# Gated attention and a low-rank mixer on one core: loads moved behind a transposition, first score pairs in two PSUM tiles, small steps in one burst

## The chip, the core and the metric

The kernel runs on one core of a Trainium2 chip. The metric is the device time of one execution in microseconds (us). The engines are called TensorE (PE in the profile, with PEld for its weight loads), VectorE (DVE), ScalarE (ACT), GpSimd (POOL) and SyncE (SP), whose queue issues nearly all DMAs.

## The reference

Batch 8, sequence S = 3136, width D = 256, key width 64, low rank 32, hidden width 1024.

```python
scores = (1.0 / S) * np.matmul(z, z.transpose(0, 2, 1))
attn = np.maximum(scores, 0.0) ** 2
x = u * np.matmul(attn, v)
h = x.transpose(0, 2, 1) @ U @ V
y = x + h.transpose(0, 2, 1)
out = y + np.maximum(y @ w_ch1, 0.0) @ w_ch2
```

The attention has no softmax: a score is scaled, rectified and squared. The low-rank part mixes over the whole sequence of a batch, so x + h of a batch can start only when all x of that batch are there. Inputs and output are fp32; the kernel's matmuls take bf16.

## The kernel before, in words

**Tiles and slots.** A batch has six groups of 512 rows (g = 0 to 5) and a small one of 64 rows (g = 6). A group is four tiles of 128 rows. The 56 pairs (batch, group) are worked one after the other, and the text calls each a slot: slot t = 7b + g. So slots 7, 14, 21, ... are the first of a batch and slots 6, 13, 20, ... the last. In slot t PE does the attention times v of its own group (`av_stream`, L644), the scores of later groups (`todo`), and, one batch behind, x + h of group t - 7 (`u2_unit`, L823) and both layers of group t - 8 (`ch1_part`, L922, and `ch2_stream`, L1010).

**Pairs over the row halves.** Nearly every matmul contracts over 64 rows, and two of them run side by side on the two halves of PE's rows, each into its own PSUM bank (`pair`, L179). A bank may pass from one half to the other only when the first has done with it; `post` (L170, the nop at L174) puts a nop on POOL that waits for that and tells PE. The loops thus run one "way" over a stretch, turn, and run the other way; score pairs are placed at the turn, where the nop is under way. A PSUM tile is two banks; there are four (`take_ps`, L148).

**Scores.** A block is 512 keys by 512 rows in bf16, made by two jobs (h = 0 and 1) of two tiles each. `score_burst` (L538) does the matmuls, `rectify` (L366) chooses who scales and rectifies (ACT by an activation, or DVE), and a square on DVE follows (`square`, L362, the instruction at L364). In slot 0 the first jobs take their way from the list `ways` (L105): "half" lets ACT take one bank and DVE the other of the same PSUM tile, each rectifying and squaring its own. For batch 0 blocks are made for both sides of the diagonal at first; later a block above the diagonal is turned by a DMA transposition (`issue_turn`, L416).

**Small group.** `score_small` (L559) makes its scores, `av_small` (L703) its attention times v, with array tiles of 64 rows by 64 columns; `ch1_small` (L968) and `ch2_small` (L1090) are its two layers, the second with 64x64 tiles too. `four_sums` (L730) adds the four partial sums of these: a copy by ACT and two adds by DVE. `last_turn` (L551) turns the small group's attention for the other groups.

**Low-rank part.** `t1_all` (L792) sums U-transposed times x over the 25 tiles of a batch, with array tiles of 128 rows by 32 columns, then an ACT copy, a DVE add and a DVE copy. `u2_unit` multiplies by V, adds x on DVE, casts the sum to bf16 (for g = 0 on DVE, L886) and issues a DMA transposition of it, `x_turn` (L782, issue L785), into u2T. `ch1_part` reads u2T.

**Order.** The order is made by a planner that runs while the program is written. Its clock counts 256 columns of a pair as one unit (109 ns in the trace). `hold(due, f)` keeps a step until the clock has passed `due`; `run_held` (L124) runs what is ripe; `urgent` keeps block turns back from the time that a sum is cast until its turn is issued. Each engine works its queue in order, SP too. In a slot `emit` (L1110) walks the light units (96 pairs of attention times v, a unit each, then the second layer's) and puts other steps in by their place: an entry (place, need, turn, step) waits for `need` free PSUM tiles, up to 14 units or `hurry` more.

**Loads.** v and z of the next batch, u of the next group and, in the first slots, U, V, w_ch1 and w_ch2 (`first_loads`) come through staging tiles and are cast a slot later (`casts_next`, held again). In slots up to 7 the loads are held at 5, 27, 49, ... units after the slot's start and u at 60.

Of the kernel before, what the change touches and what calls it, by code (L numbers as in the profile page):

```python
# [18 lines left out]
def kernel(  # L19
# [82 lines left out]
    ready_turns = []  # L102
    urgent = []
    slot = [0]
    ways = ["half", "half", "both", "dve"]  # L105
    waiting = [0]

    def needed(e):
# [257 lines left out]
    def rectify(dst, src, b, part=1, whole=False):  # L366

        ready = clock[0] + 3
        dve, act = max(free_at["dve"], ready), max(free_at["act"], ready)
        if whole and slot[0] == 0:  # L370
            dve += 6.5 * waiting[0]
            ends = {"dve": dve + DVE, "act": act + 19, "both": max(act + 8.7, dve) + 7.5}
            given = bool(ways)
            way = ways.pop(0) if ways else min(ends, key=lambda w: ends[w])
            if way == "half":
                nc.scalar.activation(out=dst[:, 0], in_=src[:, 0], func=AF.Relu, scale=scale)
                nc.vector.tensor_scalar(  # L377
                    out=dst[:, 1], in0=src[:, 1], scalar1=scale, scalar2=0.0, op0=ALU.mult, op1=ALU.max
                )
                nc.scalar.activation(out=dst[:, 0], in_=dst[:, 0], func=AF.Square)  # L380
                nc.vector.tensor_tensor(out=dst[:, 1], in0=dst[:, 1], in1=dst[:, 1], op=ALU.mult)  # L381
                done = max(book("act", ready, 5.2), book("dve", ready, 6.2))
                return done, max(book("act", ready, 5.2), book("dve", ready, 3.5))
            if way == "dve":
                if not given:
                    run_held(ready + 9)
                return one_pass(dst, src, ready)
            if way == "act":
                nc.scalar.activation(out=dst, in_=src, func=AF.Relu, scale=scale)
                nc.scalar.activation(out=dst, in_=dst, func=AF.Square)  # L390
                done = book("act", ready, 8.7)
                book("act", ready, 8.7)
                return done, free_at["act"]
        elif dve + 8 * part < act:
            nc.vector.tensor_scalar(  # L395
                out=dst, in0=src, scalar1=scale, scalar2=0.0, op0=ALU.mult, op1=ALU.max
            )
            return book("dve", ready, 11.2 if part == 1 else 6.4), None
        nc.scalar.activation(out=dst, in_=src, func=AF.Relu, scale=scale)  # L399
        return book("act", ready, 8.7 if part == 1 else 5.3), None  # L400
# [36 lines left out]
    def score_pairs(jobs):  # L437
# [50 lines left out]
            )  # L488
        return made

    def score_finish(made):
        for dst, k, ps, turn, key in made:
            if key and split(*key):
                score_finish_split(dst, k, ps, turn, key)
                continue
            if turn:
                J, g, b = turn
                unturned[blocks[b, g, J][0]] = False
            done, whole = rectify(dst, ps, key[0] if key else 0, whole=True)
            ps_free[k] = done  # L500
            waiting[0] += whole is None

            def finish(dst=dst, turn=turn, key=key, whole=whole):
                if whole is None:
                    waiting[0] -= 1
                    square(dst)
                if key:
                    squared[key] = squared.get(key, 0) + 1
                if turn:
                    hold(clock[0] + (7 if whole is None else 1), lambda: ready_turns.append(turn))  # L510

            hold(whole or done, finish)

    def score_finish_split(flat, k, ps, h, key):
# [23 lines left out]
    def score_burst(jobs):  # L538
        score_finish(score_pairs(jobs))


    def place_of(jt):

# [662 lines left out]
    def load_V(i0):  # L1206
# [27 lines left out]
        3: lambda: load_V(0),  # L1234
        4: lambda: load_V(2),
        5: lambda: load_w(0),
        6: lambda: load_w(1),
    }


# [70 lines left out]
    clock[0] = 43  # L1311
    free_at.update(dve=46, act=47)
    jobs0 = jobs_of(0, 0)
    score_burst(jobs0[:1])
    score_burst(jobs0[1:2])
    score_burst(jobs0[2:3])
    clock[0] = 60

# [1 line left out]
    for b in range(B):  # L1320
        for g in range(NQ):
            t = b * NG + g - 1
            new = jobs_of(b, g)
            if g == 0 and b > 0:
                x, y = (5, 10) if b == 1 else (5, 11)
                todo[t - 2] += new[:x]
                todo[t - 1] += new[x:y]
                todo[t] += new[y:12] if b == 1 else new[y:]
                todo[t + 1] += new[12:] if b == 1 else []
            elif b == 0 and g == 0:  # L1330
                todo[0] += new[3:]
            elif b == 0 and g and g % 2 == 0:
                todo[t] += new[:-1]
                todo[t + 1] += new[-1:]
            else:
                todo[t] += new
# [5 lines left out]
    direct = (B - 1, 0)  # L1342

    def early(b, g):
        return b > 1 and g == NQ

    for t in range(n_items):
        slot[0] = t
# [8 lines left out]
        if t + 1 < n_items and t > NG and not early(*items[t + 1]):  # L1357
            load_u(*items[t + 1])
        if t > NG and g_now == NQ and b_next < B:
            hold(clock[0] + 60 + 70, lambda b=b_next: load_u(b, NQ))  # L1360
        if t == n_items - 3:
            xTs[direct] = take_block()[1][:, : GT // 2, :].rearrange("p a (q d c) -> p (a q) d c", d=ND, c=P)
            x_turn(*direct, xTs[direct])
        for i, f in enumerate(casts_next):
            hold(clock[0] + (90 if g_now == NQ and b_next > 1 else 60 if t == NG else 15 if t >= NQ else 45) + 12 * i, f)
        casts_next = []
        spare += spare_next
        spare_next.clear()
        steps = load_part(b_next, g_now) if b_next < B else []
        steps += first_loads[t]() if t in first_loads else []  # L1370

        def load(step):
            casts_next.extend(step())
# [1 line left out]
        for i, f in enumerate(steps):  # L1375
            if t > NG:
                load(f)
            else:
                hold(clock[0] + 5 + 22 * i, lambda f=f: load(f))
        if t <= NG:  # L1380
            hold(clock[0] + 60, lambda t=t: load_u(*items[t + 1]))
        if g_now == 0 and t:
            last_turn(att[0])
        if b_next < B and g_now == 2:
# [24 lines left out]
        if av and full:  # L1409

            last = nA - 9
            for h, x, y in zip(hs, (4, 22, 36, 62), (16, 32, 48, last)):
                qc.append((x, 1, False, one(h, 0)))
                qc.append((y, 0 if y == 32 else 1, y != 32, lambda h=h, y=y: (scores(y != 32), one(h, 1)())))
            n = len(mine) - 3
            qs += [(9 + 74 * i / n, 1, False, lambda: scores(1)) for i in range(n)]
        elif av:

            if mix:
                qc += [(x, 1 - way, False, lambda way=way: ch1_small(*mix, way, box1)) for way, x in ((0, 36), (1, 48))]  # L1420
            if fin:
                qc.append((72, 2, False, lambda: (ch2_small(*fin), av_small(att[0], NQ))))
            k = min(2, len(mine) // 3)
            n = len(mine) - 3 * k
            at = [1 + 80 * i / n for i in range(n)]
            if t == 0:
                at, k = [16, 30, 46, 50, 64, 68, 78, 84, 92], 0
                qs += [(4, 0, True, lambda: scores(1)), (12, 0, True, lambda: z_turn(0, 2 * GT, on_act))]
                qs += [(x, 0, True, lambda: scores(1)) for x in (24, 40, 56, 72, 88)]
                qm.append((20, 0, False, lambda: (cast_z(2, 0, on_dve), cast_z(2, 1, on_dve), book("dve", 0, 8))))  # L1430
                qm.append((34, 0, False, lambda: z_turn(0, 4 * GT, on_act)))
                qm.append((58, 0, False, cast_tail))
                qm.append((62, 0, False, lambda: z_turn(0, 6 * GT, on_act)))
            qs += [(x, 1, False, lambda: scores(1)) for x in at]
            qs += [(x, k, True, lambda: scores(k)) for x in (16, 48, nA - 2) if k]
        else:

            small = (lambda: None) if early(*att) else (lambda: av_small(*att))
            order = mine[:1] + [small] + mine[1:]
            if mix:  # L1440
                c0, c1, d0, d1, c2, c3, d2, d3 = parts(mix, box1)
                up = [lambda: u2_unit(*u2i)]
                if fin:
                    late = mine[-1:] if early(*att) else []
                    rest = mine[: len(mine) - len(late)]
                    order = [c0] + rest[:1] + [c1, d0, d1] + [c2] + rest[1:] + [c3, d2, d3] + up
                else:
                    order = up + [small, c0, c1, d0, d1, c2, c3, lambda: t1_all(att[0]), d2, d3]
            qc += [(0, 0, False, f) for f in order]


        if av and u2i:
            if u2i[1] == 0:
                qm.append((8, 1, False, lambda: t1_all(u2i[0])))
            qm.append((22 if u2i[1] == 0 else 40, 1, False, lambda: u2_unit(*u2i)))

        if not av:
            qm += [(nC // 2, -1, False, f) for f in late or [small]] if nC else []
# [72 lines left out]
```

## Time and profile before

| | |
|---|---|
| median of 3 runs | 982.09 us (981.95 to 982.22) |
| profiled execution, own time | 986.39 us |
| its span, first to last instruction | 984.6 us |
| mean granted TensorE clock | 0.998 |
| ACT `activation` of 128x1024 from PSUM (L399), each | 1.03 us |
| DVE square of 128x1024 (L364), each | 0.69 us |
| DVE add of `u2_unit` (L870), 128x1024, each | 1.22 us |
| landing of a turn of x + h (L785), least, median, most | 2.3, 3.6, 8.4 us |

In the timeline a row has its start, its duration, the engine, the line of the kernel, the operation, what is written and read, and in square brackets the engine's idle time before it with what ended it. Rows that follow one another with one meaning are merged (x4 is four instructions). "64*128 64x256" is a matmul on an array tile of 64 rows by 128 columns whose moving operand is 64x256. A row with SPq is the time that SP's queue took to issue a DMA, not its landing. Almost all matmuls come through the helper at L184.

### The profile page before, as it was taken

To read this page: it belongs to the slowest core of one execution; us is meant where nothing else is said; L and a number is where in the kernel's file an instruction comes from. 1 tells how busy PE (TensorE), PEld (TensorE's weight loads), DVE (VectorE), ACT (ScalarE), POOL (GpSimd) and SP (SyncE) were. 2 spreads that over 40 slices of the span, in tenths; PEclk is the share of its full clock that TensorE was granted. 3 is DMA by queue.
4 is the path that set the end of the run, shared out by engine and by line. 5 is a ranking of instruction groups with operands and counts; after the bars stand their busy time and mean duration, and the time that the engine had idled before them with its cause. 6 is when DMAs were issued, how large, how long until landed. Compare 5 with 4: busy or idle time off the path is not lost.

```text
span 984.6 us, 35373 instructions
## 1 busy us (share of the span) xinstructions
PE 973.7 (99%) x16163; PEld 773.4 (79%) x16163; DVE 628.2 (64%) x811; ACT 482.4 (49%) x565; POOL 15.2 (2%) x25
## 2 busy tenths in 40 slices
PE   8999899999999999999999999999999999999998
PEld 5788677877778778787777877788777887778766
DVE  6878755668556685566755667556775567653363
ACT  7877642456324473355633555334654346431353
POOL 4200000000000000000000000000000000000000
PEclk9999999999999999999999999999999999999999
DMA  8899999979997799987999879997799978965153
GB/s 269 193 225 192 228 196 188 223 153 197 195 204 167 160 192 192 205 170 170 185 208 207 154 178 179 223 189 153 173 207 206 194 144 163 186 135 95 55 114 99
DMA packets 372405, 176.37 MB, mean 179 GB/s; under 512 B 347296, under 2 KB 350624, under 8 KB 372256
## 3 DMA queue, kind: packets, MB, share of 16 engines
q1 hardware_dynamic: 372256, 174.12, 85.6%
q8 instruction: 126, 2.06, 0.9%
q14 instruction: 23, 0.19, 0.1%
HBM read 62.56 MB, written 25.69 MB: 90 GB/s over the span
## 4 chain that ended last, share of the span: by engine, by line
PE 96%; DVE 1%; ACT 1%; DMA 1%; issue 0%; DVEq 0%
PE ps L184 93%; PE ps L714 1%; DMA u2T<-x_bf 1%; PE ps L797 1%; ACT blk L399 0%; PE ps L1096 0%; DVE blk L364 0%; PE ps L1300 0%; PE ps L331 0%; DVE blk L377 0%; DVE blk L381 0%; DVE x_bf L749 0%; DVE blk L406 0%; DVE out_sb L870 0%; DVE blk L395 0%
## 5 line engine op out<-in xcount | busy, mean ns | idle before, releaser
L184 PEld LDWEIGHTS <-blk 64*128 64x128 bf16 x12288 | 609.7, 94 | 159.9 <-POOLq L174 9.6
L184 PE MATMUL ps<-v_bf,blk 64*128 64x256 bf16 x9216 | 613.0, 269 | 2.3 <-DVE blk L364 1.1
L399 ACT ACTIVATE blk<-ps 128x1024 bf16<-128x1024 f32 (+1 forms) x335 | 315.3, 970 | 346.6 <-PE ps L184 343.2
L364 DVE TENSOR_TENSOR blk<-blk 128x1024 bf16<-128x1024 bf16 x350 | 221.1, 656 | 49.1 <-ACT blk L399 48.4
L184 PE MATMUL ps<-u2T,w_bf 64*128 64x512 bf16 (+1 forms) x1792 | 227.9, 350 | 2.8 <-DMA u2T<-x_bf 2.8
L184 PE MATMUL ps<-w_bf,blk 64*128 64x256 bf16 x3072 | 192.0, 269 | 0.0
L959 DVE TENSOR_SCALAR blk<-ps 128x1024 bf16<-128x1024 f32 x105 | 128.5, 1224 | 97.6 <-PE ps L184 96.6
L962 ACT ACTIVATE blk<-ps 128x1024 bf16<-128x1024 f32 x87 | 88.3, 1022 | 119.0 <-PE ps L184 118.8
L184 PE MATMUL ps<-zzT 64*128 64x512 bf16 (+2 forms) x902 | 129.8, 327 | 0.6 <-ACT zzT L340 0.6
L184 PEld LDWEIGHTS <-w_bf 64*128 64x128 bf16 x1792 | 84.3, 94 | 30.2 <-POOLq L174 5.0
L749 DVE TENSOR_TENSOR x_bf<-ps,u_sb 128x1024 bf16<-128x1024 f32 x48 | 58.7, 1222 | 71.4 <-PE ps L184 71.4
L870 DVE TENSOR_TENSOR out_sb<-ps,x_bf 128x1024 f32<-128x1024 f32 x42 | 51.4, 1224 | 58.1 <-PE ps L184 58.1
L1082 DVE TENSOR_TENSOR out_sb<-ps,out_sb 128x1024 f32<-128x1024 f32 x42 | 51.4, 1224 | 18.6 <-PE ps L184 18.3
L184 PEld LDWEIGHTS <-zzT 64*128 64x128 bf16 x902 | 41.2, 94 | 6.9 <-ACT zzT L340 1.5
L184 PE MATMUL ps<-t_sb,V_bf 64*128 64x256 bf16 x200 | 20.6, 269 | 0.0
L395 DVE TENSOR_SCALAR blk<-ps 128x1024 bf16<-128x1024 f32 (+1 forms) x14 | 16.6, 1185 | 5.9 <-PE ps L184 5.1
L206 DVE CAST v_bf<-stage 128x1024 bf16<-128x1024 f32 (+1 forms) x30 | 18.5, 617 | 0.0
L184 PE MATMUL ps<-v_bf,last_sb 64*128 64x256 bf16 x192 | 18.5, 269 | 0.0
L204 ACT CAST v_bf<-stage 128x1024 bf16<-128x1024 f32 (+1 forms) x18 | 18.1, 1005 | 0.0
L206 DVE CAST x_bf<-out_sb 128x1024 bf16<-128x1024 f32 x22 | 15.2, 689 | 0.3
L1082 DVE TENSOR_TENSOR blk<-ps,blk 128x1024 f32<-128x1024 f32 x5 | 6.1, 1225 | 11.9 <-PE ps L184 11.8
L204 ACT CAST x_bf<-out_sb 128x1024 bf16<-128x1024 f32 x13 | 13.5, 1037 | 0.0
(83 smaller groups left out, 239.1 us busy)
## 6 DMA issues: line engine op xcount, KB each, us to landing
u_sb<-in_u_dram SPq DMA_DIRECT2D x48, 512.0 KB, 5.1
stage<-in_v_dram SPq DMA_DIRECT2D x42, 512.0 KB, 6.1
out_dram<-out_sb SPq DMA_DIRECT2D x42, 512.0 KB, 3.1
stage<-in_z_dram SPq DMA_DIRECT2D x7, 512.0 KB, 5.9
blk<-in_v_dram SPq DMA_DIRECT2D x5, 512.0 KB, 6.3
out_dram<-blk SPq DMA_DIRECT2D x5, 512.0 KB, 2.6
blk<-blk SPq DMA_TRANSPOSE x156, 5.1
blk<-in_moe_w_ch_dram SPq DMA_DIRECT2D x4, 512.0 KB, 4.9
```

The source lines that it names most:

```text
L184: ins = nc.tensor.matmul(**args)
L204: nc.scalar.copy(out=out, in_=in_)
L206: nc.vector.tensor_copy(out=out, in_=in_)
L364: nc.vector.tensor_tensor(out=a, in0=a, in1=a, op=ALU.mult)
L395: nc.vector.tensor_scalar(out=dst, in0=src, scalar1=scale, scalar2=0.0, op0=ALU.mult, op1=ALU.max)
L399: nc.scalar.activation(out=dst, in_=src, func=AF.Relu, scale=scale)
L714: nc.tensor.matmul(out=ps[c * hp : c * hp + rows, h, :D], lhsT=smalls[b][h * hp : (h + 1) * hp, place_of(jt), :], rhs=v_bfs[b][h * hp : (h ...
L749: nc.vector.tensor_tensor(out=xs[b, g][:rows, :n, :], in0=four(box["ps"])[:rows, :n, :], in1=u_sbs[b, g][:rows, :n, :], op=ALU.mult,)
L870: nc.vector.tensor_tensor(out=o[:rows, :n, :], in0=four(ps)[:rows, :n, :], in1=x, op=ALU.add)
L959: nc.vector.tensor_single_scalar(out=r, in_=ps[:, :, :gw], scalar=0.0, op=ALU.max)
L962: nc.scalar.activation(out=r, in_=ps[:, :, :gw], func=AF.Relu)
L1082: nc.vector.tensor_tensor(out=o, in0=acc, in1=o, op=ALU.add)
```

## The change

- `ways` loses its two "half" entries. The first two score jobs go through a new function, `shared_pairs`: it takes two PSUM tiles for both jobs, and in each job ACT reads a bank of the one and DVE a bank of the other.
- Blocks of batch 0 whose first job is made in slots 1 to 5 are squared as a whole, after their second job (`whole_block`).
- Loads: w_ch2 goes from slot 6 to slot 7; slot 7's loads are held at 78, 90, 102 and 114 units, w_ch2 first; u for slot 7 is loaded 5 units into slot 6, u for slot 8 at 88 units of slot 7; u of batch 1's small group comes 2 units into slot 7, that of later batches at 60 in place of 130 units. Casts of slot 8 are held at 45 units, those of slot 7 at 15.
- `av_small` of batch 1 moves from slot 13 to place 64 of slot 7.
- In slots 14, 21, ..., 49: `ch1_small` moves from places 36 and 48 to 3 and 10; `t1_all` from place 8, and `ch2_small` with `av_small` from place 72, to one step at place 22; `u2_unit` from place 22 to 36.
- In slots 13, 20, ..., 48: x + h of the small group comes first, then the eight first-layer parts without a score between them, then scores; two score jobs instead of one stand at the second layer's turn. From batch 2 on, two score jobs come from the slot before.

The diff, cut a little at its context:

```diff
-    ways = ["half", "half", "both", "dve"]
+    ways = ["both", "dve"]
...
-            if way == "half":
-                nc.scalar.activation(out=dst[:, 0], in_=src[:, 0], func=AF.Relu, scale=scale)
-                nc.vector.tensor_scalar(
-                    out=dst[:, 1], in0=src[:, 1], scalar1=scale, scalar2=0.0, op0=ALU.mult, op1=ALU.max
-                )
-                nc.scalar.activation(out=dst[:, 0], in_=dst[:, 0], func=AF.Square)
-                nc.vector.tensor_tensor(out=dst[:, 1], in0=dst[:, 1], in1=dst[:, 1], op=ALU.mult)
-                done = max(book("act", ready, 5.2), book("dve", ready, 6.2))
-                return done, max(book("act", ready, 5.2), book("dve", ready, 3.5))
...
+    halves, merged = {}, set()
+
+    def whole_block(n, key, turn):
+        waiting[0] -= 1
+        if n == 2:
+            square(blocks[key][1], 11.7)
+            squared[key] = 2
+        if turn:
+            hold(clock[0] + 7, lambda: ready_turns.append(turn))
...
+            if key and not key[0]:
+                n = halves[key] = halves.get(key, 0) + 1
+                if n == 1 and 0 < slot[0] < NQ:
+                    merged.add(key)
+                if key in merged:
+                    finish = lambda n=n, key=key, turn=turn: whole_block(n, key, turn)
             hold(whole or done, finish)
...
+    def shared_pairs(jobs):
+
+        (ka, a), (kb, d) = take_ps(), take_ps()
+        for i, (b, g, (J, h)) in enumerate(jobs):
+            zzT = zzTs[b]
+            if h == 0:
+                blocks[b, g, J] = take_block()
+            for jj in range(2):
+                key = J * GT + 2 * h + jj
+                nc.tensor.matmul(
+                    out=(a if jj == i else d)[:, jj, :],
+                    lhsT=half(zzT, jj, key * P, P),
+                    rhs=half(zzT, jj, groups[g][0], GW),
+                    start=True,
+                    stop=True,
+                )
+            pe(GW / 256)
+            dst = blocks[b, g, J][1][:, 2 * h : 2 * h + 2, :]
+            x, y = dst[:, i], dst[:, 1 - i]
+            nc.scalar.activation(out=x, in_=a[:, i], func=AF.Relu, scale=scale)
+            nc.vector.tensor_scalar(out=y, in0=d[:, 1 - i], scalar1=scale, scalar2=0.0, op0=ALU.mult, op1=ALU.max)
+            nc.scalar.activation(out=x, in_=x, func=AF.Square)
+            nc.vector.tensor_tensor(out=y, in0=y, in1=y, op=ALU.mult)
...
-        6: lambda: load_w(1),
+        NG: lambda: load_w(1),
...
-    score_burst(jobs0[:1])
-    score_burst(jobs0[1:2])
+    shared_pairs(jobs0[:2])
     score_burst(jobs0[2:3])
...
-                x, y = (5, 10) if b == 1 else (5, 11)
+                x, y = (5, 10) if b == 1 else (5, 9)
...
     def early(b, g):
-        return b > 1 and g == NQ
+        return b > 0 and g == NQ
...
         if t > NG and g_now == NQ and b_next < B:
-            hold(clock[0] + 60 + 70, lambda b=b_next: load_u(b, NQ))
+            hold(clock[0] + 60, lambda b=b_next: load_u(b, NQ))
+        if t == NG:
+            hold(clock[0] + 2, lambda: load_u(1, NQ))
...
-            hold(clock[0] + (90 if g_now == NQ and b_next > 1 else 60 if t == NG else 15 if t >= NQ else 45) + 12 * i, f)
+            hold(clock[0] + (90 if g_now == NQ and b_next > 1 else 45 if t == NG + 1 else 15 if t >= NQ else 45) + 12 * i, f)
...
-        steps += first_loads[t]() if t in first_loads else []
+        steps = (first_loads[t]() if t in first_loads else []) + steps
...
-                hold(clock[0] + 5 + 22 * i, lambda f=f: load(f))
+                hold(clock[0] + (78 + 12 * i if t == NG else 5 + 22 * i), lambda f=f: load(f))
         if t <= NG:
-            hold(clock[0] + 60, lambda t=t: load_u(*items[t + 1]))
+            hold(clock[0] + (5 if t == NQ else 88 if t == NG else 60), lambda t=t: load_u(*items[t + 1]))
...
-                qc += [(x, 1 - way, False, lambda way=way: ch1_small(*mix, way, box1)) for way, x in ((0, 36), (1, 48))]
+                qc += [(x, 1 - way, False, lambda way=way: ch1_small(*mix, way, box1)) for way, x in ((0, 3), (1, 10))]
+            if t == NG:
+                qc.append((64, 2, False, lambda: av_small(1, NQ)))
             if fin:
-                qc.append((72, 2, False, lambda: (ch2_small(*fin), av_small(att[0], NQ))))
+                qc.append((22, 2, False, lambda: (t1_all(u2i[0]), ch2_small(*fin), av_small(att[0], NQ))))
...
-                    late = mine[-1:] if early(*att) else []
+                    late = mine[-2:] if early(*att) else []
                     rest = mine[: len(mine) - len(late)]
-                    order = [c0] + rest[:1] + [c1, d0, d1] + [c2] + rest[1:] + [c3, d2, d3] + up
+                    order = up + [c0, c1, d0, d1, c2, c3, d2, d3] + rest
...
-            if u2i[1] == 0:
+            if t == NG:
                 qm.append((8, 1, False, lambda: t1_all(u2i[0])))
-            qm.append((22 if u2i[1] == 0 else 40, 1, False, lambda: u2_unit(*u2i)))
+            qm.append((40 if u2i[1] else 22 if t == NG else 36, 1, False, lambda: u2_unit(*u2i)))
```

## The prediction

> **What bounds the kernel.** I read the page's busy shares first, then PE's own waits, then the timeline around each of them.
>
> ```profile
> span 984.6 us, 35373 instructions
> ...
> PE 973.7 (99%) x16163; PEld 773.4 (79%) x16163; DVE 628.2 (64%) x811; ACT 482.4 (49%) x565; POOL 15.2 (2%) x25
> ```
>
> TensorE (PE) is the bound; no other engine comes near. The change adds and drops no matmul, so it can win only where PE stands still or is slow. A row's duration hides small pauses, since matmuls overlap; I therefore took the distance from each matmul's start to the next in the trace. Inside a stream, a pair over both row halves of 64x256 takes 109 ns and of 64x512 216 ns; whatever is above that is a pause. All pauses add up to 17.4 us: 6.2 in the first 20 us, 1.7 from 20 to 40, 4.4 from 100 to 120, and about 0.55 in each later batch. 17.4 us is thus the ceiling. PE's waits name the large ones:
>
> ```profile
> PE ps L184 <- DMA u2T<-x_bf: 2.8, 1, 2.8
> PE ps L184 <- DVE blk L364: 1.1, 2, 0.8
> ...
> PE ps L184 <- ACT blk L380: 0.8, 1, 0.8
> ...
> PE ps L184 <- DVE blk L381: 0.2, 1, 0.2
> ```
>
> (total us, times, longest.) The first is the wait of slot 8's first `ch1_part` for the turn of x + h. The timeline there:
>
> ```profile
> 100.39 0.50 SPq L226 DMA_DIRECT2D stage<-in_z_dram  x1
> 100.94 1.09 SPq L308 DMA_DIRECT2D u_sb<-in_u_dram  x2
> ...
> 102.25 0.69 DVE L886 CAST x_bf<-out_sb 128x1024 bf16<-128x1024 f32 x1
> ...
> 102.97 2.25 SPq L785 DMA_TRANSPOSE u2T<-x_bf  x1
> ...
> 111.45 1.04 PE L184 MATMUL ps<-u2T,w_bf 64*128 64x512 bf16 x4 [2.76 <-DMA u2T<-x_bf]
> ```
>
> The turn is issued at 102.97 and lands 8.44 us later; the other 54 turns of x + h land after 2.3 to 5.7 us. From 99.10 to 101.47 five loads of 512 KB each go out just before it (two of z, one of w, two of u), and the u loads land at 107.9 and 110.5: the turn stands behind them. The windows (last columns: granted clock, DMA share, GB/s) show the sequel:
>
> ```profile
> 102.00:109.00 7.00, 6.70 (x114) 5.35 (x108) 6.24 (x11) 5.06 (x6) 0.00 (x0) 1.00 1.25 315
> 109.00:116.00 7.00, 4.54 (x46) 2.85 (x48) 2.07 (x4) 1.79 (x3) 0.00 (x0) 0.76 0.91 202
> ```
>
> After the pause the clock is at half for 3.4 us; matmuls start 213 ns apart instead of 109, which costs 1.5 us more. The place costs 2.9 + 1.5 = **4.4 us**.
>
> **Part 1: loads behind the turn.** In slot 7 the loads of w_ch2, of z and of the next u are held to 78-114 units of 256 columns (about 8.5 to 12.4 us) after the slot's start; before, z went at 5 and 27, u at 60, and w_ch2 in slot 6. By the planner the turn is ripe near 70 units (`u2_unit` about 54, from 93.9 to 99.8 us; then its own 4, a delay of 3, 11.2 and 6.3 for DVE, less 6: 72), so SP gets it ahead of them. What is left before it in SP's queue is `last_turn`, the 64 KB of u for batch 1's small group, and a u load that now goes 50 units earlier. With the usual 3.2 to 5.7 us the turn lands at 106.2 to 108.7. PE wants it at 108.5, plus 1.5 us because `av_small` of batch 1 now runs in slot 7 (50 matmuls; 1.54 us in the chain, taken out of slot 13). Gain 4.4, unless SP or DVE is 1 us later than before. The later loads have cover: w_ch2 is cast at 45 and 57 units of slot 8 and read after its 88th AV unit; at 5.2 us of landing it is there some 6 us ahead. z is turned only in slot 9. If that cover fails, PE waits for the difference.
>
> **Part 2: first pairs over two PSUM tiles.**
>
> ```profile
> 5.50 0.60 ACT L376 ACTIVATE blk<-ps 128x512 bf16<-128x512 f32 x1
> ...
> 6.13 0.69 DVE L377 TENSOR_SCALAR blk<-ps 128x512 bf16<-128x512 f32 x1 [2.29 <-ACT blk L376]
> ...
> 6.85 0.42 DVE L381 TENSOR_TENSOR blk<-blk 128x512 bf16<-128x512 bf16 x1
> ...
> 7.27 0.69 DVE L377 TENSOR_SCALAR blk<-ps 128x512 bf16<-128x512 f32 x1
> ...
> 8.00 0.86 DVE L381 TENSOR_TENSOR blk<-blk 128x512 bf16<-128x512 bf16 x1
> ```
>
> DVE reads bank 1 only when ACT has done with bank 0 of the same tile, twice (6.10 to 6.13 and 7.24 to 7.27). Both write slices of one SBUF block, but elsewhere ACT writes one half of a block while DVE squares the other without waiting, so the PSUM tile is the tie. With a tile for each, DVE starts at 5.5 and is through at 7.7 to 8.1 instead of 8.86. PE's pauses of 0.29 (at 6.93) and 0.41 us (at 8.40) are for these squares. L406 and two L364 follow on DVE's queue, and PE's start at 11.57 moves with them; the z turn at 9.24 can also come 0.6 earlier, as POOL's z casts end at 8.59. I take **0.8 us**. Bounds: 0.2, if ACT (busy 14.0 of the 16 us from 12 to 28) swallows it, to 1.2.
>
> **Part 3: whole-block squares** (batch 0, slots 1 to 5). 128x512 takes 418 ns, 128x1024 690; by that slope 2048 columns take about 1.23 us, 0.15 less than two halves. But a block's first half is squared only with its second. PE waits for squares of spilled blocks in slot 1 (0.16 and 0.15 us near 32) and not in the slots after it. I take 0, between -0.3 and +0.7 (one square later).
>
> **Part 4: one burst.** PE pauses whenever the shape of its array tiles changes:
>
> ```profile
> 334.78 0.33 PEld L184 LDWEIGHTS <-blk 64*128 64x128 bf16 x8 [0.19 <-DVE blk L959]
> ...
> 335.51 1.75 PEld L184 LDWEIGHTS <-blk 64*128 64x128 bf16 x34 [0.28 <-POOLq L174]
> ...
> 338.45 0.66 PEld L797 LDWEIGHTS <-U_bf 128*32 128x32 bf16 x25 [0.21 <-issue]
> ...
> 348.50 0.36 PEld L1096 LDWEIGHTS <-blk 64*64 64x64 bf16 x16 [0.21 <-issue]
> ...
> 350.48 0.88 PEld L184 LDWEIGHTS <-blk 64*128 64x128 bf16 x18 [0.20 <-issue]
> ```
>
> Start to start, the entries to `t1_all` (L797) and `ch2_small` (L1096) and the exits cost 89, 95, 89 and 92 ns; from `ch2_small` to `av_small`, both 64x64, nothing. The burst drops one exit and one entry, 184 ns, and adds a change from 128x32 to 64x64 that no row has: 0 to 95 ns. I take 92, as all changes seen (128x128 to 64x128 too) cost 89 to 96. Net 92 a batch.
>
> The Trainium skill (TensorEngine Tiling, Key Properties) says that a change of tiling mode, not of the tile alone, drains TensorE; it would charge that change too, so one burst wins half of what it seems to; by that rule the sum stays, and with no cost there the time would be 0.6 us lower.
>
> In the last slot of a batch the first two lines show pauses of 69 ns (second-layer matmuls waiting for the last relu) and 59 ns (POOL's nop between row halves). Two more score jobs go there: one of 216 ns stands ahead of the second layer in place of `u2_unit`'s single matmul, and two at the change of halves, longer than the 0.28 us that the nop takes. Net 128 ns. Together 0.22 us in each of six slots: **1.3 us**; bounds 0.5 to 2.2 (all four pauses and the one of 60 ns in slot 5).
>
> **Sum.** 4.4 + 0.8 + 0 + 1.3 = 6.5; I give back 0.2 for new short waits in the burst (it needs three of four PSUM tiles). The profiled execution took 986.39 us for its span of 984.6, so 980.1 in a like one. The median of the runs is 4.3 us lower by no fault of the code; 982.09 - 6.3 = **975.8 us**.
>
> **Rivals.**
> *The next x + h turn comes too late* (the other side). In slot 21 (from 337.27) `u2_unit` runs at 341.84, its turn is issued at 346.98, 2.1 us after the cast ended, behind two other turns on SP, and lands at 351.55; PE wants it at 354.20. The burst and `ch1_small` now stand before `u2_unit`: 2.0 + 0.5 us of PE, and it moves from place 26, where it found a tile, to 36 or later: 10 units, 1.1 us, so about 3.5 us. On DVE, 3.2 us of `four_sums` rows (683 + 418 + 417 ns, twice) stand before its add (1.22) and cast (0.69). Cast done about 11.5 to 12.5 us into the slot, landing 3.3 to 4.6 later: 14.8 to 17.1, wanted at 16.8. For it: the slack shrinks from 2.65 to about 1. Against: u_small's load and half of SP's wait go, and planned DMAs stay behind the turn. Late by 0.5 us in six slots: +3, 978.8; chance 0.16. Late by 2 us with the clock halved as at 111 (1.5): 6 x 3.5 = 21, 996.8; chance 0.06. It decides from 1.05 us of lateness on.
>
> The Trainium skill (TensorE: Matmul & The Clock Gate, Part 1) halves the clock only after an idle window of about 3.4 us; the trace halves it in a pause of 2.9. By the Trainium skill's rule six pauses of 2 us would cost 12, not 21: 987.8, of the same sign.
>
> *The first turn stays late*, because SP or DVE holds it: part 1 gone, 980.2; chance 0.08.
> *DVE still waits for ACT at the start* (the tie is the block): 976.6; chance 0.04.
> My own case: 0.66.
>
> **Range.** Best bounds: 4.4 + 1.5 (parts 2 and 3) + 2.2 = 8.1, 974.0, with 0.6 for measuring 973.4. Upper end 980.4, which takes in the mild late turns and the first turn that stays. About 0.2% (2 us) is what a measurement of this kernel can tell from no change: faster, below 980.1, is 0.66 + 0.16 + 0.04 and some of the 0.08; same 0.06; slower 0.07.
>
> **What would show it.** Right: no PE wait for u2T, granted clock 1.00 through 100 to 120; L377's counterpart beside ACT's; L797 and L1096 adjacent; no pauses of 59 or 69 ns in the batches' last slots. Wrong: PE waiting for u2T at the slots after 7k, or L714 for a PSUM tile; a DMA landing for slot 7's turn above 6 us; PE pauses for L364 near 30 us that grow.

## The result, and the profile after

The changed kernel takes **991.61 us** (median of 4 runs, 987.78 to 992.57) against 982.02 us for the kernel before (4 runs, 981.93 to 982.22): a ratio of 1.0085, 95% interval 1.0071 to 1.0099. By the medians it is 9.6 us slower, by the ratio 8.3; 975.8 had been predicted. The profiled execution took 990.66 us, its span 988.9. First the page's busy shares, then PE's waits (total us, times, longest):

```profile
span 988.9 us, 35333 instructions
...
PE 972.8 (98%) x16163; PEld 784.7 (79%) x16163; DVE 628.6 (64%) x795; ACT 483.0 (49%) x562; POOL 15.7 (2%) x25
```

```profile
PE ps L184 <- DMA u2T<-x_bf: 5.8, 5, 1.8
PE ps L184 <- DVE blk L364: 3.2, 3, 2.1
...
PE ps L558 <- DVE blk L569: 0.8, 1, 0.8
```

PE has as many matmuls as before and nearly the same busy time, so the loss is in pauses again, and in matmuls at half clock. The wait for u2T was one of 2.8 us and is now five that add up to 5.8; the wait for squares (L364) grew from 1.1 to 3.2, with one of 2.1; the shared PSUM tiles bring one of 0.8. Start to start, as in the prediction, all pauses add up to 21.7 us:

| pauses of PE, us | all | 0–20 | 20–40 | 40–200 | 200–920 | after |
|---|---|---|---|---|---|---|
| before, profile shown above | 17.4 | 6.2 | 1.7 | 5.0 | 3.6 | 0.8 |
| before, another execution (`e1_before_again`) | 13.5 | 6.4 | 1.7 | 0.9 | 3.7 | 0.8 |
| changed | 21.7 | 5.9 | 5.1 | 0.9 | 9.0 | 0.8 |

(Time at half clock counts as pause here.) Against the second row the change adds 8.2 us: 3.4 from 20 to 40 and 5.3 from 200 to 920, less 0.5 in the first 20. The spans, 980.6 and 988.9, differ by 8.3.

**Slot 8.** The turn that was late is on time. The windows of the same two stretches as before (last columns: granted clock, DMA share, GB/s):

```profile
102.00:109.00 7.00, 7.00 (x146) 5.85 (x142) 6.88 (x11) 5.49 (x7) 0.00 (x0) 1.00 0.53 105
109.00:116.00 7.00, 7.00 (x120) 5.43 (x114) 5.22 (x9) 3.71 (x5) 0.00 (x0) 1.00 0.91 330
```

The clock is 1.00 in both and PE never idles. The turn, issued at 106.20, lands 3.18 us later.

**Slot 1.** The timeline:

```profile
27.52 1.02 ACT L390 ACTIVATE blk<-ps 128x1024 bf16<-128x1024 f32 x1 [0.98 <-PE ps L184]
28.58 1.23 DVE L364 TENSOR_TENSOR blk<-blk 128x2048 bf16<-128x2048 bf16 x1 [1.65 <-ACT blk L390]
...
29.86 0.40 PE L184 MATMUL ps<-v_bf,blk 64*128 64x256 bf16 x2 [2.05 <-DVE blk L364]
```

DVE stands idle for 1.65 us until the block's second half is rectified, then squares all 2048 columns, and PE waits 2.05 us for it. From 29.62 the granted clock is at half for 3.41 us, which costs about 1.5 more; the window shows it (before, it had 1.00 and 7.15 us of PE work there):

```profile
26.00:34.00 8.00, 5.10 (x54) 2.98 (x52) 3.08 (x4) 3.50 (x4) 2.02 (x2) 0.79 0.57 156
```

**Slot 28**, from 457.7 us, stands for slots 14, 21, ..., 49:

```profile
465.69 0.38 PE L184 MATMUL ps<-t_sb,V_bf 64*128 64x256 bf16 x4
466.22 0.68 DVE L775 TENSOR_TENSOR u_small<-ps,u_small 64x512 f32<-64x512 f32 x1
...
467.73 1.28 DVE L364 TENSOR_TENSOR blk<-blk 128x1024 bf16<-128x1024 bf16 x2
468.93 1.21 DVE L910 TENSOR_TENSOR out_sb<-ps,x_bf 128x1024 f32<-128x1024 f32 x1
470.18 0.69 DVE L926 CAST x_bf<-out_sb 128x1024 bf16<-128x1024 f32 x1
470.20 1.24 SPq L220 DMA_DIRECT2D stage<-in_v_dram  x2
471.53 1.26 SPq L825 DMA_TRANSPOSE u2T<-x_bf  x1
...
476.40 0.61 PE L184 MATMUL ps<-u2T,w_bf 64*128 64x512 bf16 x4 [1.83 <-DMA u2T<-x_bf]
```

`u2_unit`'s matmuls run at 465.69, but DVE first does `av_small`'s sums and two squares and reaches the add only at 468.93. The cast ends at 470.87; SP then still issues a load of v, so the turn goes at 471.53, 13.8 us into the slot, and lands 4.83 us later. PE had wanted it at 474.4. Start to start these pauses are 0.67, 1.34, 1.99, 1.76, 0.80 and 0.08 us in the slots after 14 to 49: 6.6 in all. No clock is halved by them.

### The profile page after: what moved, and what is told of

Its sections match the earlier page's. It is cut to its first block, busy times and chain, and to the rows that moved or that the text cites. A ratio compares the mean times of both kernels' runs of the same rounds, so it can differ in the third digit from the quotient of the medians.

```text
span 988.9 us, 35333 instructions
## 1 busy us (share of the span) xinstructions
PE 972.8 (98%) x16163; PEld 784.7 (79%) x16163; DVE 628.6 (64%) x795; ACT 483.0 (49%) x562; POOL 15.7 (2%) x25
## 4 chain that ended last, share of the span: by engine, by line
PE 90%; DMA 4%; DVE 4%; ACT 1%; issue 1%; POOL 0%; SPq 0%; DVEq 0%; ACTq 0%; POOLq 0%
PE ps L184 88%; DMA u2T<-x_bf 2%; DVE blk L364 1%; PE ps L837 1%; PE ps L754 1%; DMA blk<-blk 1%; DMA u2T<-x_small 1%; ACT blk L390 1%; PE ps L1136 0%; DVE out_sb L910 0%; DMA blk<-in_z_dram 0%; DVE x_bf L926 0%; DVE out_sb L775 0%; DVE u_small L775 0%; ACT out_sb L773 0%
## 5 line engine op out<-in xcount | busy, mean ns | idle before, releaser
L364 DVE TENSOR_TENSOR blk<-blk 128x1024 bf16<-128x1024 bf16 (+2 forms) x331 | 218.7, 684 | 44.8 <-ACT blk L390 43.3
L999 DVE TENSOR_SCALAR blk<-ps 128x1024 bf16<-128x1024 f32 x111 | 135.9, 1224 | 114.1 <-PE ps L184 114.1
L1002 ACT ACTIVATE blk<-ps 128x1024 bf16<-128x1024 f32 x81 | 82.2, 1022 | 123.2 <-PE ps L184 119.9
L184 PEld LDWEIGHTS <-w_bf 64*128 64x128 bf16 x1792 | 88.5, 94 | 30.6 <-DMA u2T<-x_bf 7.4
L204 ACT CAST x_bf<-out_sb 128x1024 bf16<-128x1024 f32 x19 | 19.7, 1037 | 0.0
L204 ACT CAST v_bf<-stage 128x1024 bf16<-128x1024 f32 x15 | 15.6, 1037 | 0.0
L642 ACT ACTIVATE attn_small<-ps 128x512 bf16<-128x512 f32 (+1 forms) x32 | 13.1, 499 | 0.0
```

Of the source, the lines that this page charges most:

```text
L184: ins = nc.tensor.matmul(**args)
L204: nc.scalar.copy(out=out, in_=in_)
L364: nc.vector.tensor_tensor(out=a, in0=a, in1=a, op=ALU.mult)
L642: nc.scalar.activation(out=dst[:, jj], in_=src[:, jj], func=AF.Relu, scale=scale)
L999: nc.vector.tensor_single_scalar(out=r, in_=ps[:, :, :gw], scalar=0.0, op=ALU.max)
L1002: nc.scalar.activation(out=r, in_=ps[:, :, :gw], func=AF.Relu)
```

## The experiments

The theory after this result: the loss is the late turns and the whole-block squares, two separate things, and the 4.4 us of part 1 were never in the median. The rivals: the two losses share one cause (loads crowding SP), or the moved loads themselves cost the time. The experiments are called e1 to e12 and stand here by subject. Ratios are of each kernel to the kernel before on the same chip, with the 95% interval. The medians of the kernel before were 982.84, 982.09 and 982.66 us in the first (e1 to e4), second (e5, e6, e7, e9) and third (e8, e10, e11, e12) group.

**e1: the kernel before, once more** (no edit).

> The kernel before, unchanged, run again to see each execution's own span and clock. Theory A: the pause at slot 8 (2.9 us, and 1.5 us of half clock after it) stands only in some executions, the profiled one of 986.39 among them; the usual 982.0 is without it. Then executions near 982.0 have a span near 980.2 and a granted clock of 0.999 or more, and a new profile shows either 982 without a wait for u2T or 986 with it. Rival: the pause is in every execution and the profiled one was 4.3 us longer for another reason; then spans stay near 984.6 or the pause is in the profile again at a time near 982.

It took 983.73 us (1.0004, 0.9994 to 1.0014), its profiled execution 982.45 with a span of 980.6. The list of PE's waits has none for u2T; it begins with

```profile
PE ps L184 <- DVE blk L364: 1.3, 2, 0.8
```

and goes on with one each for other tiles, of 1.0 us and less. SP issues slot 7's turn no earlier than in the first profile (102.97):

```profile
103.15 1.23 SPq L785 DMA_TRANSPOSE u2T<-x_bf  x1
```

but it lands at 108.94, after 5.79 us in place of 8.44; start to start PE pauses for 0.27 us there. So the stall of 4.4 us is not in every execution, and the usual one is without it: 986.39 minus 4.4 is 982.0, the median.

**e2: halves squared one by one again.**

```diff
-                if n == 1 and 0 < slot[0] < NQ:
+                if False:
```

> The changed kernel without whole-block squares (each half is squared by itself, as before). Theory A: the pause of 2.2 us at 27.5 and the 1.5 us of half clock behind it go, and 0.3 us of waits come back: 991.6 - 3.4 = 988.2. Rival: the late turns of x + h carry the whole loss and slot 1 only moves its wait: 991 to 992.

988.01 us (1.0046, 1.0034 to 1.0059): 3.6 less than the changed kernel, and PE's pauses from 20 to 40 us fall from 5.1 to 1.7, as before.

**e3: the small steps in their old places.**

```diff
-... ch1_small(*mix, way, box1)) for way, x in ((0, 3), (1, 10))]
+... ch1_small(*mix, way, box1)) for way, x in ((0, 36), (1, 48))]
-                qc.append((22, 2, False, lambda: (t1_all(u2i[0]), ch2_small(*fin), av_small(att[0], NQ))))
+                qc.append((72, 2, False, lambda: (ch2_small(*fin), av_small(att[0], NQ))))
-            if t == NG:
+            if u2i[1] == 0:
                 qm.append((8, 1, False, lambda: t1_all(u2i[0])))
-            qm.append((40 if u2i[1] else 22 if t == NG else 36, 1, False, lambda: u2_unit(*u2i)))
+            qm.append((22 if u2i[1] == 0 else 40, 1, False, lambda: u2_unit(*u2i)))
```

> The changed kernel with the steps of slots 14 to 49 back at their old places (ch1_small 36 and 48, t1_all 8, u2_unit 22, ch2_small and av_small 72). Theory A: the six waits for u2T (0.08 to 1.99 us, 6.6 in all, and 0.3 for the small turn) go, 0.5 us of shape changes comes back: 991.6 - 6.4 = 985.2. Rival: the turns are late because of the new order of SP's queue and of slots 13 to 48, not because of the steps' places; then over 989 and PE still waits for u2T after slots 14 to 49.

985.42 us (1.0023, 1.0010 to 1.0036). No wait for u2T is left; pauses from 200 to 920 are 3.7 as before. The square's pause is there again, and this time the clock is at half for 6.83 us after it (from 28.75).

**e4: both undone** (the edits of e2 and e3).

> The changed kernel without whole-block squares and with the old places of the steps of slots 14 to 49; loads, first pairs and the order of slots 13 to 48 stay as changed. Theory A, the two losses add: 991.6 - 3.4 - 6.4 = 981.8, or up to 1 us below 982.0 by the first pairs and the last slots' cover. Rival: one of the parts left costs too, or the two losses have a common cause: 984 or more.

982.39 us (0.9992, 0.9982 to 1.0002). With e2 and e3 it makes a sum: the squares alone cost 3.0 (985.42 − 982.39), the small steps 5.6 (988.01 − 982.39), and 982.4 + 8.6 = 991.0 of 991.6. The two losses are separate, and what else the change does is worth nothing that shows in the time.

**e5: whole-block squares alone, put into the kernel before** (`halves`, `merged`, `whole_block` and the branch in `score_finish`; nothing else).

> The kernel before with whole-block squares alone. Theory A: slot 1 waits 2.2 us for the first merged square where it waited 0.16, and the clock is halved behind it: 982.8 + 3.4 = 986.2. Rival: the pause needs the earlier start that the first pairs bring; then 982.8 and the waits of 0.15 us near 32 stay.

986.77 us (1.0038, 1.0024 to 1.0052). PE's waits:

```profile
PE ps L184 <- DVE blk L364: 3.2, 3, 2.1
PE ps L184 <- DMA u2T<-x_bf: 1.2, 1, 1.2
```

The 2.1 us pause comes without any of the moved loads (the rival of loads crowding SP is out), the clock is halved from 30.89 for 3.41 us; and PE waits 1.2 us for the old turn of slot 7, which lands after 6.89 us here. By the lists it waited 2.8 us in the first profile of before and not at all in the second, nor in e8, whose loads are the old ones too (landing after 5.24 us).

**e6: `u2_unit` at place 36, no burst.** e2, with `t1_all` at 8 and `ch2_small` with `av_small` at 72.

> The changed kernel without whole-block squares; in slots 14 to 49 t1_all is back at place 8 and ch2_small with av_small at 72, while u2_unit stays at 36 and ch1_small at 3 and 10. Theory A: what makes the turn late is the small group's work in front of u2_unit (2 us of PE, 3.2 us of sums on DVE), not the place: no or little waiting for u2T, 982 to 983. Rival: the place alone is enough, since it leaves less than the turn's landing: waits as in the changed kernel, 986 or more.

982.84 us (1.0006, 0.9997 to 1.0015), and no wait for u2T. So the place alone does not make the turn late. This version lacks the burst's work on PE in front of the unit: in slot 28 `u2_unit` runs 10.8 us before PE wants its turn, in the changed kernel 8.7.

**e7: `av_small`'s sums after `u2_unit`.** e2, and:

```diff
+        def sums():
             four_sums(k, ps, u1[:rows, 1:3, :])
             nc.vector.tensor_tensor(out=xs[b, g][:rows, 0, :], in0=u1[:rows, 1, :], in1=u1[:rows, 0, :], op=ALU.mult)
...
+            later.append(sums)
...
-... lambda: u2_unit(*u2i)))
+... lambda: (u2_unit(*u2i), [f() for f in later])))
```

> The changed kernel without whole-block squares; the burst stays, but the ACT copy and the DVE sums of av_small (0.68, 0.42 and 0.42 us) are issued after u2_unit's add and cast instead of before. Theory A: DVE's queue sets the turn, the turn goes out some 1.5 us earlier, and the six waits of 5.8 us in all shrink to under 1: 988.0 - 5 = 983. Rival: PE's late u2_unit or SP's queue sets it: 986 or more.

985.92 us (1.0036, 1.0025 to 1.0048); 983 had been expected if DVE's sums were the whole cause. The waits for u2T fall from 5.8 (e2) to 3.8 us. In slot 28, which starts earlier here, the cast ends 3.66 us after `u2_unit`'s first matmul, against 5.18 in the changed kernel: 1.5 us earlier, as expected. SP becomes the last to be ready:

```profile
461.38 0.38 PE L184 MATMUL ps<-t_sb,V_bf 64*128 64x256 bf16 x4
...
464.35 0.69 DVE L933 CAST x_bf<-out_sb 128x1024 bf16<-128x1024 f32 x1
...
465.28 1.24 SPq L220 DMA_DIRECT2D stage<-in_v_dram  x2
...
466.61 1.26 SPq L832 DMA_TRANSPOSE u2T<-x_bf  x1
```

The turn is ready at 465.04 and issued 1.57 us later, behind the last rows ("tails") of v and z.

**e10: the tails later as well.** e7, and the tails are held to 115 units after the slot's start:

```diff
-                hold(clock[0] + 75, tails)
+                hold(clock[0] + (75 if b == 2 else 115), tails)
```

> The version with av_small's sums after u2_unit, and also the four loads of the last rows of z and v held to 115 units instead of 75 (batches 3 to 7), so that SP has the turn ahead of them. Theory A: with DVE relieved these loads hold the turn (1.6 us from the cast's end to the issue in slot 28); it goes out 1.5 us earlier, waits for u2T at most at slot 14: 985.9 - 3 = 982 to 983. Rival: SP is held by the blocks' turns instead; waits stay, 985 or more.

981.70 us (0.9996, 0.9987 to 1.0004): 4.2 below e7 by the medians, 3.9 by the ratios, and no wait for u2T is left. In slot 28 the cast ends at 465.39, and at once:

```profile
465.42 1.23 SPq L832 DMA_TRANSPOSE u2T<-x_bf  x1
```

So relieving DVE's queue and then SP's takes the waits away, though `u2_unit` still runs only 8.8 us before PE wants its turn: PE's later start of the unit does not by itself make the turn late. The tails moved alone, with the sums left in front, were not run. In slot 28 the changed kernel's turn stood 0.66 us behind the tails on SP and landed after 4.83 us, where e10's landed after 3.07; together that is more than the pause of 1.99, so this alone might have been enough. With both gone the burst costs nothing, and the kernel is as fast as before, not faster.

**e9: the moved loads alone, put into the kernel before** (`first_loads` at NG, the holds at 78 + 12i, u at 5 and 88, casts at 45, the order of `steps`; u of the small groups stays where it was).

> The kernel before with the loads of slots 6 to 8 alone held back. Theory A: the usual execution has no pause at slot 8 to win, so the median stays within 0.1% of before, and only executions above 985 go. Rival: the 4.4 us are won in every execution: 978.4.

983.77 us (1.0013, 1.0004 to 1.0022): slower by 1.3 us by the ratio and 1.7 by the medians, where no change had been expected. In slot 9:

```profile
122.60 0.67 ACT L204 CAST z_bf<-stage 128x576 bf16<-128x576 f32 x1 [2.32 <-DMA stage<-in_z_dram]
122.73 0.75 DVE L206 CAST z_bf<-stage 128x576 bf16<-128x576 f32 x1 [3.30 <-DMA stage<-in_z_dram]
...
124.25 1.49 PE L184 MATMUL ps<-w_bf,blk 64*128 64x256 bf16 x24 [1.03 <-ACT blk L399]
```

The casts of z's last rows stand at the head of ACT's and DVE's queues, which are idle for 2.32 and 3.30 us until the late load is there; relus and squares queue behind them, and PE pauses for 1.19 and 0.50 us (at 122.95 and 125.47). In the changed kernel's own profile the same casts wait 0.48 and 1.46 us and PE does not pause there.

**e8: shared tiles alone, put into the kernel before** (`shared_pairs`, `ways`).

> The kernel before with the first two jobs over two PSUM tiles alone. Theory A: the squares are ready 0.7 to 1.0 us earlier, but PE then stands behind POOL, whose next nop is queued behind a v cast that waits for its load (until about 9.7 us): 0 to 0.3 us gained, within 0.1% of before. Rival (as forecast): 0.8 us gained.

982.67 us (1.0007, 0.9996 to 1.0018): no difference. The changed kernel's start, with the same function, shows two waits:

```profile
5.47 0.60 ACT L568 ACTIVATE blk<-ps 128x512 bf16<-128x512 f32 x1
5.51 0.69 DVE L569 TENSOR_SCALAR blk<-ps 128x512 bf16<-128x512 f32 x1 [1.69 <-PE ps L558]
...
6.25 0.39 PE L558 MATMUL ps<-zzT 64*128 64x512 bf16 x2 [0.81 <-DVE blk L569]
...
9.72 0.61 PE L184 MATMUL ps<-v_bf,blk 64*128 64x256 bf16 x8 [0.56 <-POOLq L174]
```

ACT and DVE now read side by side. But the second job writes the other bank of a tile that DVE is still reading, and PE waits 0.81 us for it. At 9.72 PE waits for POOL's nop, which is queued behind a cast of v that waits for its load until 9.67. The profile of e8 has the 0.81 us too, but no wait for the nop. There the attention's matmuls from 7.1 to 9.9 us start 213 ns apart, and 16 of them take 1.87 us where the changed kernel's (from 7.56) take 1.05:

```profile
8.35 1.87 PE L184 MATMUL ps<-v_bf,blk 64*128 64x256 bf16 x16
```

Its record of the granted clock begins only at 10.02 us, the changed kernel's at 5.72. The same late start is in the profile of e6 (10.43) and in no other; what it does to the medians is not shown.

**e11: POOL's cast one change of halves later** (e10, and in slot 0 the cast is taken from the second change on).

> The version before in this list, and the first v cast that POOL takes in slot 0 is given one change of halves later. Theory A: the nop at 9 us no longer stands behind a cast that waits for its load; the pause of 0.72 us at 8.9 goes, 0.3 to 0.7 us less than the version before. Rival: PE waits at the next v cast or square instead: no difference.

981.94 us (0.9996, 0.9987 to 1.0005). This is no difference from e10's 981.70, as the rival said. PE's list of waits has none for POOL's nop; e10's has one of 1.2 us, but behind a cast of z whose load came at 8.49 us there and at 7.42 here, so the profiles do not show that the edit took it away.

**e12: all together** (e11; tails of batch 2 at 20 units, and steps ripe within 22 units of the end of the attention rather than 14, so that a square comes ahead of x's multiplication).

> All mended: the version before in this list, the last rows' loads of batch 2 held only 20 units (their late casts blocked ACT and DVE near 123 us in the run of the loads alone), and at the end of slot 0 one more square issued ahead of x's multiplication. Theory A: the pause of 1.0 us at 26 shrinks by 0.5 or more and slot 8 has none: 981 or lower, 0.1% below before. Rival: the square only moves the wait: as the version before.

982.40 us (0.9999, 0.9991 to 1.0008), where 981 or lower had been expected. The pause near 26 us shrinks from 1.0 to 0.89 and one of 0.34 appears. No kernel tried is measurably faster than the one before.

## Why the prediction was wrong, point by point

Three steps failed: the sum took off a stall of 4.4 us that the median did not hold; part 3 bounded the late squares at 0.7 us, and they cost 3.0; and the turns of x + h after the burst, to which the prediction's own case left about 1 us of slack, were late by 1.1 us a slot.

**Part 1 (4.4 us).** The mechanism was right: loads went behind the turn, no wait for u2T in slot 8, clock 1.00. The step that failed is the last of the sum: it carried a gain worked out for the 986.39 us execution over to the median of 982.09 and said that this median was lower "by no fault of the code". The difference of 4.3 was the very stall to be removed. With the old loads PE's pause there, start to start, is 2.9 us in the first profile of before, 0.3 in e1, 1.4 in e5 and 0 in e8. The late loads, priced at 0, measured +1.3 in e9; of that nothing is seen in the changed kernel's own profile.

**Part 2 (0.8 us).** Measured 0 (e8). The tie is the tile, as predicted, but it holds PE's writes too. In the changed kernel's profile what the squares win by an earlier start (7.8 in place of 8.9 us) ends at POOL's nop, which the prediction did not follow; in e8's own profile matmuls at half the rate stand in its place. What takes the gain in the usual execution stays open.

**Part 3 (0, bounds −0.3 to +0.7).** Measured +3.0 (e3 less e4), +3.6 (the changed kernel less e2) and, in the kernel before, +4.7 (e5, 986.77 − 982.09; 3.7 by the ratio), of which 1.2 in the profile is the wait at slot 8. The duration was exact (1.23 us). What was mis-sized is "one square later": PE waits for the first half that is now squared with the second, and the time between the halves, ACT's 1.02 us included, joins the wait. The bound had no half clock in it, which costs about 1.5.

**Part 4 (1.3 us).** Its prices of single pauses held. Entry, change of shape and exit are 89, 92 and 91 ns in slot 28 of e10, against four changes before. The last slots' pauses of 69 and 59 ns are gone (200 to 920 us: 3.65 before, 2.89 in e4; 0.76, predicted 6 × 128 ns = 0.77). The burst's own gain is small and shows in one profile only: by the pauses, e10 wins some 0.07 us a batch over e6 around the burst, 0.4 in all, and loses 0.8 in two single pauses between attention matmuls (0.56 at 223.9, 0.27 at 346.6), whose cause is open. e12 has the same burst and no such pause; its pauses from 200 to 920 us add up to 2.4, against 3.7 before. That is the 1.3 forecast, but its median (982.40 against 982.66) does not show it. The Trainium skill (TensorEngine Tiling, Key Properties) says that a change of tiling mode drains TensorE; the 92 ns from 128x32 to 64x64, which no row of before had, agree.

**The rival "the next x + h turn comes too late"** was the right one, with 0.22 for both of its sizes. Its price was 0.5 us a slot; 1.1 was measured (6.6 / 6), just above the 1.05 from which, by the prediction, it decides. It put the cast at 11.5 to 12.5 us into the slot, and slot 28 has 13.2: two squares (1.28 us) stood ahead of the add and were not counted. That half of SP's wait would go held in the changed kernel: from the cast's end to the issue it takes 0.9, 0.1, 0.7, 2.0, 0.2 and 0.0 us in slots 14 to 49, against 0.9, 2.1, 3.3, 2.4, 1.8 and 0.5 in the first profile of before. What was left out is that the tails of v and z come due just ahead of the turn: with DVE relieved (e7) SP holds it for 1.6 to 3.0 us in slots 14 to 42. The landing, taken as 3.3 to 4.6, was 4.83 in slot 28 and 3.3 to 4.8 over the six. The halved clock of its worse form did not come; the longest pause there was 2.0 us.

**The sum.** With none of the gains showing in the median (e4), the 6.3 taken off come back, and the small steps' 5.6 and the squares' 3.0 are added: 975.8 + 6.3 + 5.6 + 3.0 = 990.7 of the 991.6 measured.

## What to carry to other kernels

A stall that is seen in one profiled execution is a gain only if the median has it too: when the profile is longer than the median by just the stall's size, take a second profile before counting it. When a step is moved ahead of a transfer that lands just in time, add up everything that then stands before that transfer on each in-order queue (here DVE's squares and sums, then SP's loads); taking away one queue's share may only show the next. Merging two short instructions into one saves its overhead, but delays whoever needs the first half by all that lies between them.

## What the runs showed of the hardware

- In these traces the granted clock changes only in steps of 3.41 us: its first full stretch lasts 105.81 us, 31 steps, in the first profile of before, and 23.89 us, 7 steps, in the changed kernel, in e3 and in e5. The sum of PE's pauses within a step, counted as in the table above, went with what came next. The clock fell to half after steps with 2.59 us of pauses (before, slot 8), 2.75 (changed kernel, slot 1), 2.19 (e3) and 2.22 (e5); the steps with most pauses after which it stayed full have 2.09 (e9, from 5.46) and 1.99 (changed kernel, slot 28). So some 2.1 to 2.2 us in a step of 3.41 decided here, and the changed kernel's 2.75 holds most of the pause of 1.0 us ahead of the long one. The half clock lasted one step, and two (6.83 us) in e3, whose pause reaches 1.04 us into the second. The Trainium skill (TensorE: Matmul & The Clock Gate, Part 1) gives a free-running window of 3413 ns: the 3.41 and twice 3.41 us agree, but by its rule that a whole idle window is needed no pause here would have halved the clock.
- The same DMA transposition of x + h, issued at the same point of the same code, landed after 8.44 us in one execution, 5.79 in another (e1) and 5.24 in a third (e8, whose edit ends in slot 0).
